# Sorting two batch halves one or two units earlier on GpSimd, and tying four transposes to the last wide product

## The chip, the cores and the metric

The kernel runs on one core of a Trainium2 chip. A core has a matrix engine (TensorE, PE in the profile), a vector engine (VectorE, DVE), an activation engine (ScalarE, ACT), a general engine that also issues transfers (GpSimd, POOL), and an engine that only issues transfers here (SyncE, its queue is SPq). The metric is the device time of one execution in microseconds: the kernel before took 342.09 us, the median of 3 runs (342.05 to 342.31).

## The reference, cut to what matters

Eight batches of eight heads, 576 positions of 64 channels: attention over a window of 128 positions with a linear bias, and then a gated feed-forward block of width 1536 over all 4608 tokens.

```
scores = q @ k^T / 8 + slope[h] * -|i - j|       where 0 <= i - j < 128, else masked
attn   = softmax(scores);  a = attn @ v
x      = a with the heads side by side, 4608 x 512
out    = (silu(x @ w_gate) * (x @ w_val)) @ w_out
```

## The kernel before

**Units and ranks.** Two batches make a super-block, and a super-block has nine units of 128 query rows: four of its first batch, four of its second, and one of the two batches' last 64 rows (the tail). Units run from 0 to 35; unit 9 is the first of batch 2. A piece of q or k of 128 rows has a rank, numbered like the units: ranks 9 to 12 are batch 2, 13 to 16 batch 3, 17 the tail. The scores of a unit need k of its rank and q of its rank and, inside a batch, of the next one (line 381; 417 for the last of a batch and the tails).

**How q and k arrive.** PE contracts over partitions, so q and k must be transposed to have channels on partitions. Batches 0 and 1 are loaded in pieces and transposed on PE. From batch 2 on, `load_raw` (line 224) loads half a batch at a time, two neighbouring rows to a partition, so that the pieces in DRAM are longer; half (2, 0) is ranks 9 and 10, half (2, 1) ranks 11 and 12, and so on. In such a half the two heads of a pair and the two rows of a partition lie in the wrong order. `sort` (line 280) exchanges them in place on GpSimd with three copies (lines 285 to 287) through one small tile `aside`. The sorted half is transposed by transfers that SyncE's queue issues (`by_dma`, line 299, the transfer at line 306), one for each rank. Half (2, 0) alone is transposed on PE: `spread` (line 289) makes four groups of four transposes (line 293), two for k and two for q, which are copied to kT by ACT and to qT by DVE (line 296). The halves share a ring of six buffers (`RAW`), so a load also waits until an earlier content of its buffer has been read.

**What sets when they happen.** `loads_at(i)` (line 934) runs once after each unit's weighted products. It issues the v loads seven units ahead (line 243; four transfers for a unit of batch 2 and 3 and later, two per rank half), then sorts the halves that `sort_at` names for this unit, and then issues the loads that `load_at` names (eight units before use). GpSimd's instructions run in exactly this written order, since its queue is under a manual schedule. So a sort that is not ready holds every load behind it. Half (2, 1) is sorted at unit 7, half (3, 0) at unit 8; the loads of (3, 0) are issued at unit 5, those of (3, 1) at unit 7.

`transpose_dma` (line 911) issues transposing transfers up to a given unit: 3 units ahead up to unit 6, 4 at units 7 and 8, 5 after (line 1023). In the first super-block nothing is transposed by transfer; rank 11 of q is the first that is.

`transpose_pe` (line 904) emits PE's transposes and the spread ones (upper-case names) when the scores of the unit ahead are emitted. From there on PE's, ACT's and DVE's order is chosen by a scheduler that knows dependencies and priorities, until a written order for PE is entered at step 60 of the feed-forward block.

**The work between.** The feed-forward block of finished token blocks is interleaved with the attention units. `wide` (line 495) makes one 128-column slice of the gate or value product of a block, four matmuls of 512 columns (line 505; `pg` gate, `pv` value); they share three PSUM banks. Each `pg` goes through a tanh on ACT (`tt`, line 523) and a multiply on DVE (`uu`, line 524), each `pv` through a multiply on DVE (`hT`, line 535). `project` (line 557) makes the output of block 0, twelve matmuls into one bank `po` (line 562) that ACT copies out (line 566). Scores (`ps`, `psc`), weighted products (`av`, line 449), x transposes (`px`, line 477) and the spread transposes (`pt`) share four other PSUM banks: ACT's exponential (line 387) frees a score bank, DVE's division (line 453) a product's, ACT's copy (line 481) an x transpose's. DVE also makes sums of the output weights (`T`, lines 585 to 588) for a seven-product matrix scheme that starts with block 1's output.

Of the kernel before, what the change touches and what calls it, by code (L numbers as in the profile page):

```python
# [19 lines left out]
AHEAD = 5  # L20
SORT_AHEAD = 6
# [38 lines left out]
def kernel(  # L60
# [10 lines left out]
    nc = tc.nc  # L71
# [3 lines left out]
    NKB = DM // P  # L75
# [108 lines left out]
    last = len(units) - 1  # L184
# [3 lines left out]
    def home(name, rank):  # L188
        return kT[:, (rank + 1) % NK] if name == "k" else qT[:, rank % NQ]
# [59 lines left out]
    def transposed(name, rank):  # L249

        if rank < FIRST:
            pt = ps_f.tile([P, 4, P], FP32 if (name, rank) in hw else FP16, name="pt",
                           tag="gv" if name == "k" or rank == 1 else "po",
                           bufs=3 if name == "k" or rank == 1 else 1)
        else:
            pt = ps_a.tile([P, 4, P], FP16, name="pt", tag="a")
        if (name, rank) in hw:

            for _ in range(IDLE[(name, rank)]):
                nc.tensor.matmul(pt.rearrange("p j t -> p (j t)"), idle[:, 0:P], idle,  # L260
                                 start=True, stop=True)
            for j in range(4):
                nc.tensor.transpose(pt[:, j, :], hw[(name, rank)][:, j * P:(j + 1) * P], idf)
            nc.vector.tensor_copy(home(name, rank), pt)
            return
        t_ = nat_of.pop((name, rank))

        for j in range(4):
            nc.tensor.transpose(pt[:, j, :], t_[:, 2 * j:2 * j + 2, :],
                                idm if rank < FIRST else idm2)  # L270
        if name == "k" and rank >= FIRST:
            nc.scalar.copy(home(name, rank), pt)
        else:
            nc.vector.tensor_copy(home(name, rank), pt)

    def in_pairs(name, half):

        return raw[name, half].rearrange("p h t d -> p (h t d)").rearrange("p (j t c) -> p j t c", j=4, t=RUN)
# [10 lines left out]
    def spread(name, t):  # L289

        pt = ps_a.tile([P, 4, P], FP16, name="pt", tag="a")
        for j in range(4):
            nc.tensor.transpose(pt[:, j, :], in_pairs(name, (2, 0))[:, j, t, :], idm2)
        w = P // RUN
        to = (kT if name == "k" else qT)[:, 0:RUN, :, w * t:w * t + w]
        (nc.scalar.copy if name == "k" else nc.vector.tensor_copy)(
            to.rearrange("p c j q -> p j c q"), pt.rearrange("p j (c q) -> p j c q", c=RUN))

    def by_dma(name, rank):

        to, c = home(name, rank), rank % 9
        if c == 8:
            nc.sync.dma_start_transpose(to, nat_of.pop((name, rank)).rearrange("p h d -> p (h d)"))
            return
        half, r0 = (2 * (rank // 9) + c // 4, c % 4 // 2), P // RUN * (c % 2)
        nc.sync.dma_start_transpose(
            to.rearrange("p j (t q) -> p (j t) q", t=RUN),
            in_pairs(name, half)[r0:r0 + P // RUN].rearrange("p j t c -> p (j t c)"))
# [6 lines left out]
    raw_order, dma_order, dma_need = [], [], [0] * 9  # L315
# [12 lines left out]
        dma_need.append(len(dma_order))  # L328

    ex = {}  # L330
    scored = [False]
    begun = {}

    def begin_scores(i, q4, par, pool=None, tag="a", bufs=4):
# [94 lines left out]
    def weighted(i):  # L429

        s, p = units[i]
        x = xpool.tile([P, H, D], FP16, name="x", tag="x", bufs=4)
        xs[i] = x
        for half in range(2):
            pool, tag = (ps_f, "gv") if i < FIRST else (ps_a, "a")
            av = pool.tile([P, 4, D + 1], FP32, name="av", tag=tag)
            todo = []
            for j in range(4):
                h = 4 * half + j
                if p == 8:  # L440
                    for n, kt in enumerate((3, 7, 8)):
                        todo.append((j, ex[(s, "c", n)][:, slot(h), :], va[9 * s + kt][:, h, 0:D + 1]))
                else:
                    if p not in (0, 4):
                        todo.append((j, ex[(s, p - 1)][:, slot(h), 128:256],
                                     va[9 * s + p - 1][:, h, 0:D + 1]))
                    todo.append((j, ex[(s, p)][:, slot(h), 0:128], va[9 * s + p][:, h, 0:D + 1]))
            for n, (j, w, val) in enumerate(todo):
                nc.tensor.matmul(av[:, j, :], w, val, start=(n == 0), stop=(n == len(todo) - 1))  # L449
            rec = xpool.tile([P, 4, 1], FP32, name="rec", tag="rec", bufs=3)  # L450
            with tc.high_priority() if i in (6, 7) else ExitStack():
                nc.vector.reciprocal(rec, av[:, :, D:D + 1])
                divided[i] = nc.vector.tensor_mul(x[:, 4 * half:4 * half + 4, :], av[:, :, 0:D],  # L453
                                                  rec.broadcast_to([P, 4, D]))

    xT = {}
# [38 lines left out]
    def wide(n, m, which, c1=512):  # L495

        w, ms = wg_sb if which == "g" else wv_sb, slice(m * P, (m + 1) * P)
        ps, c0 = early.pop((n, m, which), (None, 0))
        if ps is None:
            pool, tag, bufs = ((ps_a, "a", 4) if (n, m, which) in OTHER  # L500
                               else (ps_f, "po", 1) if (n, m, which) == (0, 3, "g")
                               else (ps_f, "gv", 3))
            ps = pool.tile([P, 512], FP32, name="p" + which, tag=tag, bufs=bufs)
        for kb in range(NKB):
            nc.tensor.matmul(ps[:, c0:c1], w[:, kb, ms], xT[n][:, kb, c0:c1],  # L505
                             start=(kb == 0 and c0 == 0), stop=(kb == NKB - 1 and c1 == 512),
                             skip_group_check=(n <= 1))
        if c1 < 512:
            early[(n, m, which)] = (ps, c1)
        return ps  # L510
# [393 lines left out]
    def transpose_pe(n):  # L904
        nonlocal done_pe
        while done_pe < n:
            name, rank = pe_order[done_pe]
            (spread(name.lower(), rank) if name.isupper() else transposed(name, rank))
            done_pe += 1

    def transpose_dma(n):
        nonlocal done_dma
        while done_dma < n:
            by_dma(*dma_order[done_dma])
            done_dma += 1

    def transposes_to(i):
        transpose_pe(pe_need[min(i, 9)])
        transpose_dma(dma_need[min(i, last)])
# [3 lines left out]
    def use_of(which):  # L923
        name, half = which
        return 9 * half + 8 if name == "tail" else first_rank(half[0]) + 2 * half[1]

    def sort_at(which):
        r0 = use_of(which)
        return {11: 7, 13: 8}.get(r0, r0 - SORT_AHEAD)

    def load_at(which):
        return use_of(which) - LOAD_AHEAD
# [17 lines left out]
    def run(steps):  # L950
        for fs in steps:
            for f in fs:
                f()
            yield
# [42 lines left out]
    def attention():  # L997

        waiting = []
        transposes_to(FIRST)  # L1000
        for _ in run(scores(FIRST)):
            yield FIRST
        for i in range(FIRST, last + 1):
            late = i >= LATE
            if i < last:
                transposes_to(i + 1)
                for n, _ in enumerate(run(scores(i + 1))):
                    yield i - len(waiting)
                    if n == 2 and late:
                        weighted(i)  # L1010
                        yield i - len(waiting)
            if not late or i == last:
                weighted(i)
                yield i
            loads_at(i)
            if i == 4:
                nc.sync.dma_start(dist_s, dist_s_d.ap())
            if i == 7:
                later_masks(dist_s)
            if i == 8:  # L1020
                make_mask(4)
                make_mask(5)
            transpose_dma(dma_need[min(i + (AHEAD if i > 8 else 4 if i > 6 else 3), last)])
            yield i - len(waiting)
            if late and i < X_DMA_FROM:
                if waiting:
                    x_transposed(waiting.pop(0))
                waiting.append(i)
                yield i
                yield i  # L1030
                continue
            while waiting:
                x_transposed(waiting.pop(0))
            x_transposed(i)
            yield i
            yield i + 1
# [56 lines left out]


    att = attention()
    done = n_att = 0
    ready = [4, 8, 13, 17, 22, 26, 31, 35, 36]
# [88 lines left out]
```

## Time and profile before

| | |
|---|---|
| median of 3 runs | 342.09 us (342.05 to 342.31) |
| the profiled execution | 342.63 us |
| its span, first to last instruction | 340.9 us |
| PE busy in the span | 327.2 us (96%) |
| DVE busy | 276.8 us (81%) |
| ACT busy | 207.4 us (61%) |
| POOL busy | 133.3 us (39%) |
| granted PE clock, mean | 0.994 of full |
| kraw, qraw loads (256 KB each), issue to landing, median | 7.9 and 6.0 us |

How to read the profile: times are microseconds from the start of the span. A timeline line gives start, duration, engine, source line, operation, output<-input, and in brackets how long the engine was idle before and what ended that. A line of waits gives the total, the number of times, the longest. A transfer's timeline line is the time that the issuing queue spent on it, not the transfer itself; from its issue to its landing is a separate figure. A matmul's duration includes its latency, so the work of a group is read from start to start. A wait for several events is put down to the one that came last in the profile.

### The profile page before, as it was taken

The numbers are of one execution on the slowest core, as the hardware profiler recorded it, in microseconds if no ns is written. First come the engines' busy times: TensorE is split into PE (matmuls) and PEld (weight loads), VectorE is DVE, ScalarE is ACT, GpSimd is POOL, SyncE is SP. The second block draws the span as 40 slices with busy tenths as digits, with TensorE's granted clock in tenths as the row PEclk, the third lists the DMA queues.
The fourth block names the chain that finished last, engine by engine and source line by source line (L and its number), as shares of the span: only waits on it lengthen the run. The fifth ranks groups of instructions, "written<-read, shape, count | busy, mean of one in ns | idle before, by whom it ended". The sixth has DMA issues, their size and how long they took to land. (4 is left out here: it accounts for less than half of the span.)

```text
span 340.9 us, 7793 instructions
## 1 busy us (share of the span) xinstructions
PE 327.2 (96%) x2931; PEld 217.3 (64%) x2931; DVE 276.8 (81%) x643; ACT 207.4 (61%) x417; POOL 133.3 (39%) x210
## 2 busy tenths in 40 slices
PE   8999998969999999899999999999999999999995
PEld 3664464434456665456665665666688888888884
DVE  4678967959979769998899999999956785775592
ACT  4976688426576566465565646563366776676650
POOL 8967768799469459646409100000000000000000
PEclk9999999979999999999999999999999999999999
DMA  9999999999999999999999944024202112022024
GB/s 153 168 180 176 176 192 161 112 136 183 169 162 106 172 191 123 191 162 139 101 189 156 133 95 92 17 47 62 63 2 64 30 33 64 0 64 51 13 63 123
DMA packets 140885, 38.49 MB, mean 113 GB/s; under 512 B 128560, under 2 KB 136496, under 8 KB 140848
## 3 DMA queue, kind: packets, MB, share of 16 engines
q0 software_dynamic: 94304, 18.62, 72.5%
q1 hardware_dynamic: 45856, 18.76, 35.6%
q10 hardware_dynamic: 688, 0.62, 0.6%
q8 instruction: 23, 0.38, 0.5%
q14 instruction: 14, 0.11, 0.1%
HBM read 37.98 MB, written 9.44 MB: 139 GB/s over the span
## 5 line engine op out<-in xcount | busy, mean ns | idle before, releaser
L505 PE MATMUL pv<-xT,wv_sb 128*128 128x512 f16 (+2 forms) x312 | 77.3, 366 | 0.2
L505 PE MATMUL pg<-xT,wg_sb 128*128 128x512 f16 (+2 forms) x324 | 77.0, 356 | 0.1
L523 ACT ACTIVATE tt<-pg 128x512 f16<-128x512 f32 x68 | 40.9, 603 | 46.3 <-PE pg L505 45.8
L387 ACT ACTIVATE ex<-ps 128x512 f16<-128x512 f32 x96 | 50.2, 606 | 11.4 <-PE ps L381 11.3
L524 DVE SCALAR_TENSOR_TENSOR uu<-tt,pg 128x512 f16<-128x512 f16 x67 | 45.6, 680 | 8.6 <-ACT tt L523 8.3
L535 DVE TENSOR_TENSOR hT<-uu,pv 128x512 f16<-128x512 f16 x68 | 46.1, 679 | 2.1 <-PE pv L505 0.4
L243 POOL DMA_DIRECT2D va<-in_v_dram x56 | 40.3, 749 | 16.6 <-PE av L449 14.4
L505 PEld LDWEIGHTS <-wv_sb 128*128 128x128 f16 x312 | 28.0, 98 | 25.8 <-issue 3.5
L642 PEld LDWEIGHTS <-hT 128*128 128x128 f16 x384 | 37.1, 98 | 11.0 <-DVE hT L596 0.6
L505 PEld LDWEIGHTS <-wg_sb 128*128 128x128 f16 x324 | 28.6, 98 | 23.4 <-issue 2.1
L393 DVE TENSOR_TENSOR ex<-ex,m_reg 128x1024 f16<-128x1024 f16 x42 | 29.0, 696 | 6.6 <-ACT ex L387 6.6
L642 PEld LDWEIGHTS <-S 128*128 128x128 f16 x288 | 27.5, 98 | 8.5 <-issue 2.2
L453 DVE TENSOR_TENSOR x<-av,rec 128x256 f16<-128x256 f32 x72 | 28.4, 418 | 0.4
L642 PE MATMUL po<-T,hT 128*128 128x256 f16 x192 | 26.2, 273 | 0.3 <-DVE hT L596 0.3
L642 PE MATMUL po<-T,S 128*128 128x256 f16 x192 | 25.9, 273 | 0.3 <-ACT u2s L668 0.3
L421 ACT ACTIVATE exc<-psc 128x512 f16<-128x512 f32 x40 | 21.4, 605 | 2.5 <-PE psc L417 2.4
L787 DVE TENSOR_TENSOR hT<-s,v 128x512 f16<-128x512 f16 x18 | 7.6, 423 | 17.7 <-ACT s L786 17.7
L381 PE MATMUL ps<-qT,kT 64*128 64x256 f16 x192 | 16.7, 278 | 4.7 <-DMA qT<-qraw 3.5
L449 PEld LDWEIGHTS <-ex 128*128 128x128 f16 x384 | 17.5, 97 | 4.5 <-issue 1.2
L449 PE MATMUL av<-va,ex 128*128 128x65 f16 x384 | 19.3, 193 | 0.5 <-ACT ex L387 0.3
L381 PEld LDWEIGHTS <-kT 64*128 64x128 f16 x192 | 7.8, 95 | 16.5 <-issue 8.5
L733 PEld LDWEIGHTS <-wg_sb 128*128 128x128 f16 x144 | 14.1, 98 | 1.8
(156 smaller groups left out, 592.2 us busy)
## 6 DMA issues: line engine op xcount, KB each, us to landing
out_dram<-osb SPq DMA_DIRECT2D x50, 128.0 KB, 2.4
va<-in_v_dram POOLq DMA_DIRECT2D x56, 64.0 KB, 7.3
kraw<-in_k_dram POOLq DMA_DIRECT2D x12, 256.0 KB, 7.9
qraw<-in_q_dram POOLq DMA_DIRECT2D x12, 256.0 KB, 6.0
out_dram<-osb SPq DMA_DIRECT2D x8, 256.0 KB, 6.5
wg_sb<-in_moe_w_gate_dram POOLq DMA_DIRECT2D x6, 256.0 KB, 7.7
wo_sb<-in_moe_w_out_dram POOLq DMA_DIRECT2D x3, 512.0 KB, 8.2
wv_sb<-in_moe_w_val_dram POOLq DMA_DIRECT2D x5, 256.0 KB, 8.1
```

Of the source, the lines that this page charges most:

```text
L243: nc.gpsimd.dma_start(va[rank][n:n + P // run, :, 0:D], src[t])
L381: nc.tensor.matmul(two[par][:, j, :], kT[rows, ks, pair, :], qT[rows, p:p + 2, pair, :], start=(j == 0 and not early_tile), stop=(j == 1))
L387: nc.scalar.activation(e[:, o:o + 2, :], banks[q4][par], AF.Exp, scale=scale)
L393: nc.vector.tensor_mul(e[:, o, :], e[:, o, :], reg[:, o, :])
L421: nc.scalar.activation(er4[:, :, par], banks[par].rearrange("k (a b) q -> k a b q", a=2), AF.Exp, scale=scale)
L449: nc.tensor.matmul(av[:, j, :], w, val, start=(n == 0), stop=(n == len(todo) - 1))
L453: divided[i] = nc.vector.tensor_mul(x[:, 4 * half:4 * half + 4, :], av[:, :, 0:D], rec.broadcast_to([P, 4, D]))
L505: nc.tensor.matmul(ps[:, c0:c1], w[:, kb, ms], xT[n][:, kb, c0:c1], start=(kb == 0 and c0 == 0), stop=(kb == NKB - 1 and c1 == 512), skip_ ...
L523: nc.scalar.activation(tt, pg[:, c0:c1], AF.Tanh, scale=0.5)
L524: nc.vector.scalar_tensor_tensor(out=uu, in0=tt, scalar=one if (n, m) == PIN else 1.0, in1=pg[:, c0:c1], op0=ALU.add, op1=ALU.mult)
L535: product_of[n, m] = nc.vector.tensor_mul(hT[n][:, m, c0:c1], acted[(n, m)][1][:, c0:c1], pv[:, c0:c1])
L642: nc.tensor.matmul(dst, a[:, m, cols], b[:, m, :], start=(start and m == 0), stop=(m == HM - 1), skip_group_check=True)
```

## The change

Half (2, 1) is sorted at unit 5 instead of 7, and half (3, 0) at unit 7 instead of 8. The unit's place in `loads_at` is after its v loads and before its q and k loads, so on GpSimd the sort of (2, 1) comes ahead of the loads of (3, 0), and the sort of (3, 0) ahead of the loads of (3, 1). Up to unit 6 the transposing transfers are emitted four units ahead instead of three. `wide` remembers its last matmul, and the spread transposes on PE are ordered behind that matmul (`issue_after` adds an order between instructions of one engine and no wait between engines).

```diff
-    scored = [False]
+    scored, last_wide = [False], [None]
...
         for kb in range(NKB):
-            nc.tensor.matmul(ps[:, c0:c1], w[:, kb, ms], xT[n][:, kb, c0:c1],
-                             start=(kb == 0 and c0 == 0), stop=(kb == NKB - 1 and c1 == 512),
-                             skip_group_check=(n <= 1))
+            last_wide[0] = nc.tensor.matmul(
+                ps[:, c0:c1], w[:, kb, ms], xT[n][:, kb, c0:c1],
+                start=(kb == 0 and c0 == 0), stop=(kb == NKB - 1 and c1 == 512),
+                skip_group_check=(n <= 1))
...
             name, rank = pe_order[done_pe]
-            (spread(name.lower(), rank) if name.isupper() else transposed(name, rank))
+            if name.isupper():
+                with tc.issue_after(last_wide[0].ins):
+                    spread(name.lower(), rank)
+            else:
+                transposed(name, rank)
...
     def sort_at(which):
         r0 = use_of(which)
-        return {11: 7, 13: 8}.get(r0, r0 - SORT_AHEAD)
+        return {11: 5, 13: 7}.get(r0, r0 - SORT_AHEAD)
...
-            transpose_dma(dma_need[min(i + (AHEAD if i > 8 else 4 if i > 6 else 3), last)])
+            transpose_dma(dma_need[min(i + (AHEAD if i > 8 else 4), last)])
```

On the engines the instructions are the same in kind and number; their order differs. On PE it differs between 52 us and about 95 us of the profile before: the sixteen spread transposes and unit 9's scores stand later among the wide products and projections, and after that stretch both orders are the same. ACT's and DVE's orders differ in the same stretch. On GpSimd the two sorts stand earlier, as told above. On SyncE's queue one transfer of q and one of k in half (3, 0) exchange places.

## The prediction

> **What bounds the kernel now.** I read the page's slices first (TensorE, PE, is at 8 or 9 tenths nearly everywhere, its clock below full only in slice 9), then the busy time by stretches, PE's waits, and the timelines of PE, GpSimd (POOL) and SyncE's queue (SPq) around the one hole.
>
> ```profile
> 65.00:70.00 5.00, 2.33 (x14) 1.04 (x12) 4.14 (x10) 1.68 (x3) 4.59 (x9) 1.00 1.74 106
> 70.00:75.00 5.00, 4.19 (x18) 1.69 (x19) 2.03 (x4) 2.06 (x4) 4.69 (x10) 0.66 1.58 161
> 75.00:80.00 5.00, 5.00 (x40) 2.48 (x38) 4.81 (x12) 2.07 (x4) 4.58 (x10) 1.00 1.74 171
> ```
> The second column is PE's busy time, then weight loads, VectorE (DVE), ScalarE (ACT), POOL, and PE's granted clock. PE is idle for half of 65-70, runs at clock 0.66 after it, and is full again from 75.
>
> ```profile
> PE ps L381 <- DMA qT<-qraw: 3.5, 1, 3.5
> PE pt L293 <- POOL qraw L286: 0.9, 1, 0.9
> ```
> These are two of PE's three longest waits; the third (1.2, at the start) is not touched. After 92 us none is over 0.6. So PE's order is the bound, and what leaves these waits reaches the end unless later inputs stop it.
>
> ```profile
> 54.09 0.40 PE L293 MATMUL pt<-idm,qraw 128*128 128x128 f16 x4 [0.86 <-POOL qraw L286]
> 66.73 0.59 PE L505 MATMUL pg<-xT,wg_sb 128*128 128x512 f16 x2
> 70.81 1.03 PE L381 MATMUL ps<-qT,kT 64*128 64x256 f16 x8 [3.48 <-DMA qT<-qraw]
> 71.78 1.89 PE L505 MATMUL pv<-xT,wv_sb 128*128 128x512 f16 x4
> 73.46 3.14 PE L562 MATMUL po<-wo_sb,hT 128*128 128x512 f16 x12
> ...
> 79.61 0.61 PE L381 MATMUL ps<-qT,kT 64*128 64x256 f16 x8
> 80.15 1.04 PE L505 MATMUL pv<-xT,wv_sb 128*128 128x512 f16 x4
> 81.02 2.75 PE L562 MATMUL po<-wo_sb,hT 128*128 128x512 f16 x12
> ```
> The same three groups stand twice: start to start, 0.97, 1.68 and 2.98 after the hole (the next group starts at 76.44), against 0.54, 0.87 and 2.59 (next 83.61) at full clock. The hole costs 3.48 and then 5.63 - 4.00 = 1.63 us of slow clock.
>
> ```profile
> 49.14 0.88 POOL L230 DMA_DIRECT2D qraw<-in_q_dram  x1 [1.22 <-PE psc L417]
> 50.56 0.88 POOL L230 DMA_DIRECT2D kraw<-in_k_dram  x1 [0.55 <-PE psc L417]
> ...
> 57.55 1.36 POOL L243 DMA_DIRECT2D va<-in_v_dram  x2 [0.39 <-PE ps L381]
> 59.31 0.89 POOL L230 DMA_DIRECT2D qraw<-in_q_dram  x1 [0.40 <-DMA qraw<-in_q_dram]
> 61.73 0.88 POOL L230 DMA_DIRECT2D kraw<-in_k_dram  x1 [1.54 <-PE pv L505]
> 62.60 2.74 POOL L243 DMA_DIRECT2D va<-in_v_dram  x4
> 65.29 0.45 POOL L285 COPY aside<-qraw 128x256 f16<-128x256 f16 x1
> 65.81 0.40 POOL L286 COPY qraw<-qraw 128x256 f16<-128x256 f16 x1
> 66.27 0.40 POOL L287 COPY qraw<-aside 128x256 f16<-128x256 f16 x1
> ```
> ```profile
> 66.69 3.05 SPq L306 DMA_TRANSPOSE qT<-qraw  x2
> ```
> The hole's chain: the sort of q's half (2,1) ends at 66.67, its first transposing transfer (rank 11) is issued at 66.69 and lands 4.1 us later, and unit 10's scores start. The half was in SBUF long before: issued at 49.14 it landed after 9.9, near 59.1. Its sort stood behind two loads and four v transfers.
>
> **The change, part by part.** *Sort of (2,1) at unit 5.* It now stands behind the v transfers of 57.55, ahead of the loads of (3,0). q's sort starts when q has landed, 59.3 (the load at 59.31 now waits for the same event), and takes 1.38 (65.29 to 66.67): 60.7. k landed after 10.6, 61.2 to 61.7 (the load at 61.73 waits on that landing's semaphore; the profile's PE label is the last event it saw); sorted at 63.1. SP has nothing ahead of rank 11, so it issues at 60.75, 5.9 earlier, and lands between 64.9 (the 4.1 of before) and 69.7 (8.9, the longest of this kernel's raw and tail transposes). PE wants it at 68.4 (step d below). I take 5.0, the row of rank 12: 65.8, no wait; the far end gives 1.3.
>
> *Queued behind it on POOL.* The loads of (3,0) move from 59.31/61.73 to 63.1/64.0, four v transfers follow to 67.6, then comes (3,0)'s sort, now one unit earlier, in front of (3,1)'s loads. It waits for landings: 5.5 and 5.8 in before, so 68.6 and 69.8; sorted by 71.3 instead of 74.5. Then (3,1)'s loads at 71.3/72.2 (before 68.22/69.19), two pairs of v transfers to 76, landings (before 4.9, 7.1) by 79.3, sorted at 77.6 and 80.7 (before 77.5, 79.0), rank 15's transfer at 78-79 (before 78.77). So POOL ends some 2 us late against before while PE is 4 early. Slack: unit 14 is the first to need rank 15, at 96.21 before, so near 92; landing (8.9 at most) by 88. Tail loads end near 84, batch 4's first loads at 85 (83.05 before), their transposes by 108 at most, wanted at 119.8 - 4. At 117.4 POOL waits 5.6 us for PE's release of a v tile: there it is in step again. Cost 0, covered by those 4 us; without them PE would wait for the difference.
>
> *Transfer four units ahead.* Rank 11's q alone is emitted one unit earlier; SP's queue has nothing to pass (its last issue was at 1.88) and it waits for its sort anyway. Cost and gain 0. The other differences on SP are one swap, inside batch 3's first half.
>
> *Spread transposes behind the last wide product.* This takes the 16 transposes and unit 9's scores from 52-57 to behind the pg of 62. The 0.86 wait goes: the sorted half was ready at 54.5. Six later projection matmuls and three more come forward. Up to the pg that starts at 76.70, PE issues the same matmuls in both, so only waits differ. Walking the new order with the old rows: (a) the second projection reuses the one `po` bank and so waits for ACT's copy: xT copy 53.08, mask copy 53.54, osb 54.11 to 54.72, PE ready at 54.4: 0.4. (b) Spread at 61.9 to 62.8; ACT's two kT copies end at 63.7, DVE's two qT copies (0.42 each) at 64.15; PE, after six more matmuls, is at 64.1: 0.15. (c) All four banks of the attention pool then hold unit 9's scores, so unit 8's two weighted products wait for exp 0 and 1 (0.60 each): 0.5. (d) Unit 8's x is ready 0.2 after PE, which puts unit 10's first scores at 68.4; their last two matmuls wait for a bank that ACT frees with the xT copy after an exp: 0.9. Sum 2.15.
>
> Bounds for (a) to (d): 0, if fillers hide all of them, and twice the sum, 4.3, if each slips a step; I take the walk. They stay under 1 us each; the 0.86 hole left the clock at 1.00 in 50-60, so I add no slow clock.
>
> *DVE.* It is full in 75-80 (4.81 of 5.00). At the pg of 76.70 it has two ex multiplies (0.69) still to do and one weight sum (0.57) done early, 0.8 behind; walking its rows on, unit 11's x is ready at 82.7 against 86.74, 4.0 earlier, just PE's gain. So DVE allows 4.0 and no more.
>
> *GpSimd beside DVE.* The sorts now run against DVE's multiplies at 59-63. Row: L585 takes 0.75, 0.9 each for the two that start at 74.95 beside a sort; four such ops at 0.15 make 0.6 of DVE time, inside (a)-(d)'s bounds. [...]
>
> **Sum.** Removed 0.86 + 3.48 + 1.63 = 5.97; added 2.15; gain 3.8, and 4.0 by DVE's walk. I take 4.0. The profiled execution took 342.63 with a span of 340.9; its span becomes 336.9 and it 338.6. The median shown is 342.09, 0.54 lower: 338.1.
>
> **The rivals.** *R1, the gain is half eaten (0.13):* (a)-(d) come out near twice the walk, or rank 11 lands after 8.9. For it: four banks shared by spread, scores and products, DVE full. Against: every bank's releaser is a 0.6 op. 5.97 - 4.3 = 1.7, with the 1.3 of the late landing 0.4: 340.4 to 341.7.
>
> *R2, no change (0.04):* the gained time is lost again at a later DMA. For it: DMA at 9 tenths until 220 us. Against: no later DMA wait of PE. 342.1.
>
> *R3, slower (0.11): POOL stands in (3,0)'s sort.* With the longest landings of before, 9.9 and 10.6, q lands at 73.0, k at 74.6, sorted at 76.0, (3,1)'s q is issued then, lands at 85.9 behind the v transfers, is sorted at 87.3 and transposed by 96.2 (8.9), while unit 14 wants it at 92: 4.2 of hole, 1.6 of slow clock, 338.1 + 5.8 = 343.9. It decides once rank 15 lands after 92. For it: the 10 us landings were real at 49-61, and three of them must now follow each other. Against: that was under 180-200 GB/s of weights; the loads of 59-69 took 4.9 to 7.1.
>
> **How the numbers follow.** Forecast (0.72): its own range is 336.4 (most of (a)-(d) hidden: gain 5.7) to 339.9 (gain 2.2). The range reaches into R1, to 341.0; outside lie R2, R3 and an edge of R1, about 0.2. Faster than 0.2% (0.7 us, what a measurement can tell): 0.72 + 0.13 = 0.85; same 0.04; slower 0.11.
>
> **What would show it.** Right: no PE wait for `qT<-qraw` near 68; clock 1.00 in 65-75; the rank 11 transfer issued at 60.5-61; small PE waits on ACT and DVE of 2 us in all in 54-71; the pg of 76.70 near 72.7. Wrong: PE waiting for a transposed rank 11, 13 or 15; the L296 copies or the xT copy holding PE over 1 us each; a clock under 1.00 anywhere in 55-95; or DVE's x near 83 late by more than 1 us.

## The result, and the profile after

| | before | after |
|---|---|---|
| median | 342.05 us (342.01 to 342.31, 5 runs) | **345.69 us** (344.13 to 349.99, 5 runs) |
| the profiled execution, its span | 342.63, 340.9 us | 346.06, 344.3 us |
| granted PE clock, mean | 0.994 | 0.990 |
| PE busy in the span | 327.2 us | 328.9 us |

The ratio is 1.0087 [1.0057, 1.0116]: the change costs 0.9%, where 1.2% less time was forecast. Medians here and below count every run; a ratio compares the means of the fast runs alone, so this one leaves out the slow run of 349.99. From line 506 on, line numbers after are one higher, past line 913 five.

Busy time by stretches, after (second column PE, then weight loads, DVE, ACT, POOL, clock):

```profile
65.00:70.00 5.00, 4.64 (x48) 2.22 (x47) 5.00 (x12) 2.90 (x6) 3.31 (x5) 1.00 1.79 147
70.00:75.00 5.00, 5.00 (x35) 2.09 (x33) 4.45 (x11) 4.07 (x8) 3.50 (x6) 1.00 1.60 150
```

The hole of 65 to 70 and the clock of 0.66 behind it are gone. PE's waits, after:

```profile
PE psc L417 <- DVE rec L452: 2.5, 1, 2.5
PE po L563 <- DMA wo_sb<-in_moe_w_out_dram: 1.7, 1, 1.7
PE pg L505 <- DMA xT<-x: 1.5, 1, 1.5
```

`qT<-qraw` (3.5) and `POOL qraw` (0.9) have left the list, and these three are new at its head. PE's timeline, after, says where:

```profile
54.53 1.02 PE L563 MATMUL po<-wo_sb,hT 128*128 128x512 f16 x4 [1.65 <-DMA wo_sb<-in_moe_w_out_dram]
...
73.41 1.02 PE L505 MATMUL pg<-xT,wg_sb 128*128 128x512 f16 x4
...
133.62 1.04 PE L505 MATMUL pg<-xT,wg_sb 128*128 128x512 f16 x4 [1.46 <-DMA xT<-x]
...
169.65 0.21 PE L417 MATMUL psc<-qT,kT 64*128 64x128 f16 x1 [2.53 <-DVE rec L452]
170.55 0.60 PE L417 MATMUL psc<-qT,kT 64*128 64x128 f16 x7 [0.69 <-DVE x L453]
171.09 1.89 PE L505 MATMUL pg<-xT,wg_sb 128*128 128x512 f16 x4
```

The pg that started at 76.70 before starts at 73.41: PE leads by 3.3 us, and still by 2.8 at 131. Setting the same matmul of both traces side by side, the lead falls to 1.2 at 133.6, climbs back to 2.5 by 166, and PE is 0.2 behind at 169.65 and 1.1 behind at 170.55. Behind the two idle stretches the same four matmuls take 1.89 instead of 1.04, and the clock (third number from the end) is below full for ten microseconds:

```profile
170.00:175.00 5.00, 4.45 (x34) 2.79 (x35) 5.00 (x13) 2.07 (x4) 0.19 (x1) 0.50 1.60 178
175.00:180.00 5.00, 5.00 (x31) 2.35 (x29) 3.98 (x11) 1.35 (x3) 0.00 (x0) 0.83 1.35 216
```

At 190 PE is 3.6 behind, and the span ends 3.4 later (344.3 against 340.9).

The wait at 169.65 is named after DVE, which was itself held. DVE's timeline, after:

```profile
169.08 0.42 DVE L453 TENSOR_TENSOR x<-av,rec 128x256 f16<-128x256 f32 x1 [4.42 <-DMA xT<-x]
```

From unit 16 on, x is transposed by transfers (line 471). The pg that waits at 133.62 is the first to need unit 16's, the first of these transfers. And x has four tiles, so unit 24, whose division this is, may not write its x until the transfer that reads unit 20's, the fifth, has landed. Both losses therefore wait for one kind of transfer, `xT<-x`. It is issued on SyncE's queue, whose timeline before was:

```profile
113.40 2.51 SPq L306 DMA_TRANSPOSE qT<-qraw  x2
116.02 3.48 SPq L306 DMA_TRANSPOSE kT<-kraw  x2
119.59 1.01 SPq L554 DMA_DIRECT2D out_dram<-osb  x2
120.69 5.30 SPq L471 DMA_TRANSPOSE xT<-x  x2
...
150.60 2.52 SPq L306 DMA_TRANSPOSE qT<-qraw  x2
153.21 1.47 SPq L471 DMA_TRANSPOSE xT<-x  x1
```

and after:

```profile
117.44 2.99 SPq L306 DMA_TRANSPOSE qT<-qraw  x2
120.54 2.64 SPq L306 DMA_TRANSPOSE kT<-kraw  x2
123.27 1.21 SPq L555 DMA_DIRECT2D out_dram<-osb  x2
124.57 2.90 SPq L471 DMA_TRANSPOSE xT<-x  x2
...
157.76 3.74 SPq L306 DMA_TRANSPOSE qT<-qraw  x2
161.60 1.35 SPq L471 DMA_TRANSPOSE xT<-x  x1
```

The x transfers come 3.9 and 8.4 us later, each directly behind the raw halves' transfers, and those come at the end of a sort on GpSimd. POOL's timeline shows the same half before (112.05) and after (116.09), first before:

```profile
106.04 0.89 POOL L230 DMA_DIRECT2D qraw<-in_q_dram  x1
...
112.05 0.40 POOL L285 COPY aside<-qraw 128x256 f16<-128x256 f16 x1 [1.50 <-DMA qraw<-in_q_dram]
```

then after:

```profile
85.91 0.96 POOL L230 DMA_DIRECT2D qraw<-in_q_dram  x1
...
109.07 0.89 POOL L230 DMA_DIRECT2D qraw<-in_q_dram  x1
...
116.09 0.40 POOL L285 COPY aside<-qraw 128x256 f16<-128x256 f16 x1 [2.51 <-DMA qraw<-in_q_dram]
```

POOL was 2.9 us late already at the first load of batch 4 (85.91 against 83.05), and stays late: load, landing, sort and next load follow one another. Ahead of unit 20's transfer the load of the half is issued 3.6 late (146.63 against 143.07), lands after 8.7 us instead of 6.1, and its sort starts 6.2 late (155.47 against 149.25).

**The sums.** The first x transfer landed 5.8 after its issue before, at 126.5, and PE wanted it at 134.84: a slack of 8.3. After, it is issued 3.9 later, lands after 9.0 (3.2 more), and PE is ready 2.7 early (132.16): 9.8 - 8.3 = 1.5, and the wait is 1.46. Unit 20's before: issued 153.21, landed 4.5 later at 157.7, DVE at 167.07: 9.4. After: 8.4 later, 7.4 to landing (2.9 more), and DVE is ready 2.4 early (164.66): 13.7 - 9.4 = 4.3, and the wait is 4.42.

### The profile page after: what moved, and what is told of

It reads as the page before. It is cut to its first block, busy times and chain, and to the rows that moved or that the text cites. A ratio compares the mean times of both kernels' runs of the same rounds, so it can differ in the third digit from the quotient of the medians.

```text
span 344.3 us, 7791 instructions
## 1 busy us (share of the span) xinstructions
PE 328.9 (96%) x2931; PEld 218.5 (63%) x2931; DVE 277.1 (80%) x643; ACT 207.1 (60%) x417; POOL 136.7 (40%) x210
## 5 line engine op out<-in xcount | busy, mean ns | idle before, releaser
L505 PE MATMUL pg<-xT,wg_sb 128*128 128x512 f16 (+2 forms) x324 | 78.3, 359 | 1.5 <-DMA xT<-x 1.5
L381 PE MATMUL ps<-qT,kT 64*128 64x256 f16 x192 | 15.9, 272 | 0.6 <-DVE qT L274 0.5
L749 ACT COPY p<-gY 128x512 f32<-128x512 f32 x18 | 10.5, 585 | 7.6 <-PE gY L734 7.3
```

The source lines that it names most:

```text
L505: last_wide[0] = nc.tensor.matmul(ps[:, c0:c1], w[:, kb, ms], xT[n][:, kb, c0:c1], start=(kb == 0 and c0 == 0), stop=(kb == NKB - 1 and c1 ...
```

## The experiments

The first suspects were the sorts, which now stand ahead of loads on POOL, and the tie of the spread transposes, which changes PE's order and what it frees when. The third idea came from their runs: whatever makes POOL late, it is the written order on SyncE's queue that carries the lateness to x. Each expectation tells the theories as they stood then.

Where nothing else is said, an edit is against the changed kernel.

**Each part alone.** `spread_only` keeps the tie, with the sorts and the look-ahead of before:

```diff
-        return {11: 5, 13: 7}.get(r0, r0 - SORT_AHEAD)
+        return {11: 7, 13: 8}.get(r0, r0 - SORT_AHEAD)
...
-            transpose_dma(dma_need[min(i + (AHEAD if i > 8 else 4), last)])
+            transpose_dma(dma_need[min(i + (AHEAD if i > 8 else 4 if i > 6 else 3), last)])
```

> The new PE, DVE and ACT order (spread tied to the last wide product) with GpSimd's old order: sorts at units 7 and 8, transfers 3 ahead. Theory 1 (the early sorts stand in front of loads, so each later load, sort and transposing transfer is late, and the x transposes behind them on SyncE's queue are late): no PE wait on xT near 133 and no DVE wait on xT near 165; the hole for rank 11 stays, 1 to 3 us; time 341 to 343.5. Theory 2 (the new PE order is itself what meets the later waits, whatever GpSimd does): holes after 130 us remain, 2 us or more in all; time 344 to 347.

Measured: 345.94 us, ratio 1.0105 [1.0047, 1.0164]. Without the early sorts the hole at 70 is gone too (PE reaches those scores at 69.72, where before it wanted them at 67.3), and the loss is there in full. PE's timeline of this kernel, and POOL's:

```profile
137.61 1.89 PE L505 MATMUL pg<-xT,wg_sb 128*128 128x512 f16 x4 [5.74 <-DMA xT<-x]
```
```profile
71.67 0.89 POOL L230 DMA_DIRECT2D qraw<-in_q_dram  x1 [4.20 <-DMA qT<-qraw]
...
87.97 0.96 POOL L230 DMA_DIRECT2D qraw<-in_q_dram  x1
```

Here POOL is late by another way: the load of half (3, 1) takes over a buffer of the ring that a late transposing transfer still reads. The first load of batch 4 is at 87.97, the first x transfer is issued at 126.86. So the early sorts alone are not the cause.

`sorts_only` keeps the sorts and the look-ahead, and drops the tie:

```diff
-                with tc.issue_after(last_wide[0].ins):
-                    spread(name.lower(), rank)
+                spread(name.lower(), rank)
```

> The old PE, DVE and ACT order with GpSimd's new order (sorts at units 5 and 7) and transfers 4 ahead. Theory 1: rank 11 no longer holds PE near 67, so PE leads by 3 to 5 us at 100 us, and then the late x transposes take it back: a PE or DVE wait for an xT transfer between 125 and 175, 2 us or more; time 342 to 346. Theory 2: the old PE order keeps the lead of 3 to 5 us to the end, no xT wait; time 337 to 339.5.

Measured: 343.62 us, ratio 1.0055 [1.0025, 1.0085]. PE leads by 5.0 us at 75, still by 4.8 at 130, and then loses it in one place; PE's timeline of this kernel:

```profile
134.35 1.89 PE L505 MATMUL pg<-xT,wg_sb 128*128 128x512 f16 x4 [4.11 <-DMA xT<-x]
```

The first load of batch 4 is at 88.73, the first x transfer at 124.89. So the tie alone is not the cause either: each part makes POOL late, and each ends at the same transfer.

**One sort back.** `after_13at8` sorts half (3, 0) at unit 8 again.

```diff
-        return {11: 5, 13: 7}.get(r0, r0 - SORT_AHEAD)
+        return {11: 5, 13: 8}.get(r0, r0 - SORT_AHEAD)
```

> The changed kernel with half (3,0) sorted at unit 8 again, so that the loads of (3,1) go out ahead of that sort; PE, DVE and ACT order as in the changed kernel. Theory 1: GpSimd issues the loads of (3,1) 2 us or more earlier than the changed kernel's 71.5 and 73.6, stays less late at 100 to 150 us, the xT waits shrink to under 1 us in all, and the gain of about 3 us at 100 us stays: 338.5 to 340.5. Rival (GpSimd's lateness at 100 to 165 comes from slow landings and PE's lead there, not from where the first sorts stand): GpSimd is as late at 119 and 149 as in the changed kernel within 1.5 us and the waits stay: 343 to 347.

Measured: 347.07 us, ratio 1.0117 [1.0046, 1.0188]. Its profiled execution took 554 us at a mean clock of 0.561, so its waits tell nothing. The other three (344.04, 346.00 and 348.14) show no gain from it; why is open.

**A fifth tile for x.** `after_x5` takes away only DVE's wait, with every engine's order as in the changed kernel.

```diff
-        x = xpool.tile([P, H, D], FP16, name="x", tag="x", bufs=4)
+        x = xpool.tile([P, H, D], FP16, name="x", tag="x", bufs=5)
```

> The changed kernel with five x tiles instead of four; every engine's order is the same. The DVE wait of 4.4 us near 165 (an x tile whose transposing transfer is late) goes, since the tile wanted is then the one of a unit earlier; with it the PE waits of 2.5 and 0.7 and the slow clock. If these are the whole second loss: 339.5 to 341. The PE wait of 1.5 near 133 stays (that is a product waiting for xT itself). If the time stays above 343, the loss sits elsewhere.

Measured: 342.63 us, ratio 1.0028 [0.9995, 1.0061]. DVE's wait at 169 is gone, and PE's waits behind it; PE's wait for the first x transfer stays (2.7 at 134.34, and a clock of 0.66 in 135-140). In this trace PE's lead falls from 3.3 to -0.2 there and stays about that to the end, so the first wait, with its slow clock, is enough to eat the lead. In the changed kernel's own trace the second is the dearer one: it took PE from 2.5 ahead to 3.6 behind, the first 1.5. What the fifth tile is worth in time is not shown: the step from 1.0087 to 1.0028 is no larger than the changed kernel's own spread (`after_again`, below).

**The control.** `before_again` is the kernel before, on the chip of the next runs.

> The kernel before, once more, for its trace on this chip. If the lateness of GpSimd in the variants is theirs and not the chip's: loads of (4,0) near 83, of (5,0) near 106, the first xT transfer near 121, no PE wait on xT; 341 to 343.5.

Measured: 343.90 us once, span 342.1. The first load of batch 4 is at 83.07, the first x transfer at 121.59, and PE has its hole of 3.67 and no wait for xT. The lateness belongs to the changed kernels, not to a chip.

**SyncE's order, and nothing else.** `after_xt_first` orders each raw half's transposing transfer behind the last x transfer that the program has emitted. PE, DVE, ACT and POOL keep the changed kernel's order.

```diff
+    last_x = [None]
...
-            nc.sync.dma_start_transpose(dst, x)
+            last_x[0] = nc.sync.dma_start_transpose(dst, x)
...
-            by_dma(*dma_order[done_dma])
+            with tc.issue_after(last_x[0].ins) if last_x[0] else ExitStack():
+                by_dma(*dma_order[done_dma])
```

> The changed kernel with the raw halves' transposing transfers tied, on SyncE's queue, behind the last x transpose emitted before them; order on PE, DVE, ACT and GpSimd is the same. Theory 3 (PE's lead is lost because the x transposes stand in SyncE's queue behind transfers of raw halves whose sort GpSimd has not done): the first xT transfer is issued near 118 instead of 124.6 and that of unit 20 near 153 instead of 161.6, the waits on xT near 133 and 165 go, and the lead of about 3 us at 130 stays to the end: 338.5 to 340.5. Rival (the x transposes are late because the transfers themselves land slowly, or the raw halves tied behind them now hold the scores): PE or DVE still waits 2 us or more for a transfer after 120 us: 342.5 to 347.

Measured: **339.16 us, ratio 0.9908 [0.9874, 0.9942]**. Its SyncE queue, where the x transfer now stands ahead of the half's transfers, which follow from 122.63:

```profile
113.81 2.60 SPq L556 DMA_DIRECT2D out_dram<-osb  x3
116.50 1.70 SPq L472 DMA_TRANSPOSE xT<-x  x1
122.63 1.20 SPq L306 DMA_TRANSPOSE kT<-kraw  x1
```

its GpSimd, which is later still than in the changed kernel (85.91):

```profile
87.94 0.96 POOL L230 DMA_DIRECT2D qraw<-in_q_dram  x1
```

and PE's longest waits:

```profile
PE po L564 <- DMA wo_sb<-in_moe_w_out_dram: 1.7, 1, 1.7
PE nil L172 <- DVE kT L122: 1.2, 1, 1.2
PE ps L382 <- DVE x L454: 0.7, 2, 0.5
```

No wait for xT is left on PE or DVE, and a lead of 2.9 to 3.6 us goes through to the end (span 337.7). The transfer still takes 9.2 us to land: an earlier issue covers it. This settles how the lateness reached PE.

**Both remedies.** `after_xt_first_x5` adds the fifth x tile to it (the two edits above together).

> As the run before, and five x tiles instead of four. Theory 3: within 0.7 us of the run before, since the tile wait is already gone. If the x tiles hold by themselves, 1 us or more below it.

Measured: 339.27 us, ratio 0.9898 [0.986, 0.9936]: nothing more to gain, so the x tiles were only short because the transfer was late.

**Loads ahead of sorts.** `after_loads_first` moves the loop over loads in `loads_at` ahead of the loop over sorts, to cure GpSimd's lateness at its source.

```diff
-        while sorted_ < len(raw_order) and i >= sort_at(raw_order[sorted_]):
-            if raw_order[sorted_][0] != "tail":
-                sort(*raw_order[sorted_], nc.gpsimd)
-            sorted_ += 1
...
+        while sorted_ < len(raw_order) and i >= sort_at(raw_order[sorted_]):
+            if raw_order[sorted_][0] != "tail":
+                sort(*raw_order[sorted_], nc.gpsimd)
+            sorted_ += 1
```

> The changed kernel with the loads of q and k ahead of the sort at every unit, so that a sort that waits for its half holds no load behind it. If GpSimd's lateness (2 to 6 us between 85 and 158 in the changed kernel) comes from sorts that stand in front of loads: loads of (4,0) at 83 or before, of (5,0) at 106 or before, first xT transfer near 121, no wait on xT over 1 us: 338.5 to 340.5. If it comes from slow landings and from buffers that come free late: loads no earlier than the changed kernel's 85.9 and 109.1, waits on xT stay: 342.5 to 347.

Measured: 345.24 us, ratio 1.0055 [1.0014, 1.0096]. The first loads are a little earlier (half (3, 0) at 58.51 against 61.44), but (3, 1)'s waits 2.87 at 69.82 for `DMA qT<-qraw`, as a buffer of the ring is not free yet, and the sorts behind it wait with it: the first load of batch 4 is at 90.11, later than in the changed kernel (85.91). PE waits 3.4 for xT, 1.6 for qT, 1.1 for kT. The idea did not work.

**The cure without the change, and with each part.** `before_xt_first`, `sorts_xt_first` and `spread_xt_first` add the SyncE edit to the kernel before, to `sorts_only` and to `spread_only`.

> The kernel before with the raw halves' transposing transfers tied on SyncE's queue behind the last x transpose. Theory 3: it has no wait on xT to lose, so the time stays within 0.7 us of before (341.3 to 343), with the hole for rank 11 of 3.5 us still there; so the new SyncE order alone is not what made the changed kernel with it faster. If it gains 2 us or more, that order helps by something else.

> Sorts at units 5 and 7, old PE order, with x transposes first on SyncE's queue. Theory 3: the lead of 5.0 us that the sorts alone had at 130 us stays: 336.5 to 338.5, a little below the changed kernel with the same tie (339.2). If a transfer still holds PE after 120 us: 340 or more.

> Old sorts, spread transposes tied to the last wide product, with x transposes first on SyncE's queue. Theory 3: the lead of 3.1 us of that kernel stays: 338.3 to 340.3. If the late (3,1) loads (71.7, behind a buffer that comes free late) hold the scores instead: a wait on qT or kT of 1 us or more, 340.5 or more.

Measured, in one table with the runs above:

| | SyncE order as it was | x transfers first |
|---|---|---|
| neither part | 342.24 | 341.84, ratio 0.9993 [0.9972, 1.0014] |
| sorts early | 343.62, 1.0055 [1.0025, 1.0085] | **337.89, 0.9872 [0.9856, 0.9887]** |
| spread tied | 345.94, 1.0105 [1.0047, 1.0164] | 340.38, 0.9944 [0.9926, 0.9962] |
| both (the change) | 345.69, 1.0087 [1.0057, 1.0116]; again, 343.09, 1.0004 [0.9975, 1.0034] | 339.16, 0.9908 [0.9874, 0.9942] |

The kernel before took 342.05, 342.11 and 342.24 in these measurements, and each ratio is to its own. The edit alone gives nothing: before, no x transfer was late for anyone. With it each part gains, and the sorts alone gain the most, 342.24 - 337.89 = 4.35 us; with the tie added, 1.27 of that is lost. The two ranges of times just meet (337.60 to 338.00 without the tie, 337.77 to 339.43 with it), but PE's lead at the end agrees, 4.8 against 3.1. Sorts and SyncE's order together are the fastest version found, clearly ahead of both kernels.

PE's waits in `sorts_xt_first`, the first four:

```profile
PE nil L172 <- DVE kT L122: 1.2, 1, 1.2
PE pt L293 <- POOL qraw L286: 0.9, 1, 0.9
PE px L478 <- DVE x L454: 0.7, 1, 0.7
PE ps L382 <- DVE x L454: 0.7, 2, 0.5
```

The 0.9 that the tie was to remove stays, the wait of 1.7 for `wo_sb` that the tie brings is not there, and neither is the hole.

**The changed kernel again.** `after_again`, on the second chip:

> The changed kernel once more, on the chip of the three above, for its spread of times and a second trace: 344 to 346.5, a PE wait on xT of 1 to 4 us near 133 in its trace, a lead over before of 2.5 to 3.5 us ahead of it.

Measured: 343.09 us (340.37 to 346.31, 10 runs), ratio 1.0004 [0.9975, 1.0034], below the range expected. In its profiled execution (343.62) the three waits stand as before, one a little shorter; its waits of PE:

```profile
PE psc L417 <- DVE rec L452: 2.5, 1, 2.5
PE po L563 <- DMA wo_sb<-in_moe_w_out_dram: 1.7, 1, 1.7
...
PE pg L505 <- DMA xT<-x: 1.0, 1, 1.0
```

POOL is a little less late (first load of batch 4 at 85.56, first x transfer at 123.29 against 124.57), and PE leads by 2.4 where it led by 1.2. The clock after the long wait falls less, too: 0.70 in 170-175 and 1.00 after, against 0.50 and 0.83. So the size of the loss varies (all runs of the changed kernel lie between 340.4 and 350.0 us, those with the SyncE edit between 337.8 and 339.4); on this chip the change is not measurably slower, but it gains nothing, for the same reason.

## Why the prediction was wrong

**What came out.** Rank 11's transfer is issued at 59.73 (60.75 forecast), the hole and its slow clock are gone, and the 0.86 too. Rank 11 lands in time. The pg of 76.70 starts at 73.41 (72.7 forecast): 3.3 of the 4.0.

**A term that was left out.** Part (a) priced ACT's copy of `osb` ahead of the second projection at 0.4; no wait of PE for it stands in the list. The dear wait of this stretch comes earlier: the last four matmuls of the first projection, which the tie brings forward, need the last load of w_out. It was issued at 43.73 and landed at 54.49, and PE waited 1.65 for it. Before, the same load landed at 54.78, and the spread transposes and their 0.86 wait stood in front of those four matmuls, which ran from 54.83 on. For (b) to (d), forecast at 1.75 together, the list has one wait of 0.2. So the total came out near (the sum was off by 0.7) by luck: a wait that the walk did not have stood in for those that hardly came. By the prediction's own terms the tie was a net loss, 2.15 added for the 0.86 that it removes; on top of the sorts it cost 1.27 in the table.

**The DVE and GpSimd terms.** DVE's x for unit 11 was forecast for 82.7; PE waits 0.93 for it until 84.34, where it started at 86.80 before, so the lead is down to 2.5 there, and 2.8 from 100 on. Beside half (3, 1)'s sort a multiply took 0.89 against 0.69, and three sums 0.88, 0.61 and 0.61 against 0.74 and twice 0.41: 0.7 of the 1.6; the rest is open.

The sort of (2, 1) ran at 58.3 to 61.5 beside DVE. One weight sum took 0.88 there against 0.74, one sum of hT 0.66 against 0.42 (0.4 together, where the prediction had put four weight sums at 0.15 each, 0.6), and one of the six copies 0.74 instead of 0.40 to 0.47. In (3, 0)'s sort three copies took 0.90, 0.74 and 0.74, and two of DVE's multiplies 0.88 and 0.78 against 0.69. Beside these two sorts together the four DVE instructions took 0.7 us more. All four (`T<-wo_sb,one`, `S<-hT` and two of `ex<-ex,m_reg`) have both inputs in SBUF, while `uu<-tt,pg` and `hT<-uu,pv`, which read one input from PSUM, took 0.65 to 0.69 in both traces, beside a sort or not. Why is not shown.

**The step that failed** is "Queued behind it on POOL ... So POOL ends some 2 us late against before while PE is 4 early ... Cost 0, covered by those 4 us". Its walk of POOL was good: it put (3, 1)'s sorts at 77.6 and 80.7, rank 15's transfer at 78 to 79 and batch 4's loads at 85; the trace has 78.52 and 81.85 for the ends of the sorts, 78.55 and 85.91. Its slack was not. It was checked for the scores, which need the transposed halves, and these did arrive in time. It was not checked for what stands behind those transfers on SyncE's queue, the stores and the x transfers, which wait for nothing of POOL's and have slacks of 8.3 and 9.4 us. Take off the 4 us by which PE was to be early, and 4.3 and 5.4 were left, with 2 forecast for POOL's lateness, and nothing for two things that a walk to 85 cannot show: the lateness does not end and grows (2.9 at 85.91, 1.8 at 98.13, 3.0 at 109.07, 4.7 at the load of 120.28), and the landing takes 3 us longer. The remark that POOL is "in step again" at 117.4 failed as well: the v transfers there are in step, but q's and k's loads stand ahead of them in the written order.

**The rivals.** R2 (the gained time is lost at a later DMA) named the kind of event and got 0.04, on the argument that PE had no later DMA wait before (its row for it, DMA at 9 tenths, holds until 196 us in the page's slices, not 220). That argument shows only that slack was not below zero; what counted was how much above zero it was. R3 had the right sign and began with the right thing, GpSimd standing in a sort, but waited at the wrong place (unit 14 for rank 15, which landed in time). None of them reached x. The clock makes up most of the loss: PE is 1.1 behind after its waits at 170.55 and 3.6 behind at 190, so 2.5 us come from the slow clock behind 3.2 us of idling.

## What to carry to other kernels

When work moves on one engine, list what it feeds, and then everything that stands behind those consumers in every queue that issues in written order; price for each the slack, the later issue, the longer landing and the lead of the one who waits. A transfer whose data is ready belongs ahead of one that still waits for a slow engine: this order alone was worth 3.9 us here on one chip (343.09 to 339.16), 6.5 against the first measurement, and nothing measurable before the change. A wait that is zero in the trace says nothing of the slack behind it.

## What the runs showed of the hardware

On SyncE's queue a transfer that waited held those behind it: the x transfer was issued at 124.57 in the changed kernel, behind transfers that wait for a sort, and at 116.50 in `after_xt_first`, where it was ordered ahead of them.

The same x transfer landed 4.9 to 5.8 us after its issue in three profiles of the kernel before (one with the SyncE edit), and 8.7 to 10.7 in ten profiles of kernels with either part or both (all but the one at a clock of 0.561). In the changed kernel 256 KB loads of q and k (120.28 and 121.16) and four v transfers (122.03) go just ahead of it; before, the loads were at 115.62 and 116.49 and the v transfers came after it. In `after_xt_first` the q and k loads (111.18 and 112.05) are as far ahead of the x transfer (116.50) as they were before, and it still landed only after 9.2; the v transfers (112.92) are ahead of it there too, which makes them the nearer suspect. That this traffic is the cause was not tried by itself.

PE's clock behind its idle stretches, as the mean of a slice of 5 us: 1.00 after idling of 1.46 and 1.65 (both in the changed kernel), 0.66 after 2.68 (`after_x5`) and after the 3.48 of before, and 0.50 after 2.53 and 0.69 with one matmul between (the changed kernel); after the same two stretches in `after_again` it was 0.70. So the same idling gave two clocks; what decides between them is not shown.
